# Projections, kv and num of a fused attention and feed-forward kernel in stationary tiles of 32 columns

## The chip, the cores and the metric

One core of a Trainium2 chip runs the whole program. The metric is the device time of one execution in microseconds. A second number of the same kind is the time of one execution that the hardware profiler recorded; the trace and all views of the profile come from that one execution.

## The reference

Linear attention with random features, followed by a gated feed-forward layer, all in float32. There are 8 batches with 8 heads, 576 positions a head, 64 numbers a head and 128 random features:

```python
def phi(x):                                   # x = q * scale or k * scale
    proj = np.einsum('bhsd,md->bhsm', x, omega)
    sq = np.sum(x * x, axis=-1, keepdims=True) / 2.0
    h = proj - sq
    h = h - np.max(h, axis=-1, keepdims=True)
    return np.exp(h) / np.sqrt(m)
q_p, k_p = phi(q_s), phi(k_s)
kv = np.einsum('bhsm,bhsd->bhmd', k_p, v)
z = np.sum(k_p, axis=2)
num = np.einsum('bhsm,bhmd->bhsd', q_p, kv)
den = np.einsum('bhsm,bhm->bhs', q_p, z)[..., None] + 1e-06
...
out = ((x @ w_a) * (x @ w_b)) @ w_out         # x = num / den, 4608 x 512, d_ff = 1536
```

## The kernel before, in words

**Two kinds of work on TensorE.** The feed-forward layer takes most of it. Its matmuls use the full array, 128 rows by 128 stationary columns, with each number split into a high and a low part; lines 1057, 1127, 1247 and 1340 in the profile are these. Between them stand short bursts of attention work in plain float32, for one pair of heads at a time (32 pairs in all, 4 per batch). The change touches these bursts.

**Projections.** The queries and keys of a pair lie with the 64 numbers of a head on the partitions: one head on partitions 0 to 63 and the other on 64 to 127, positions along the free dimension. A chunk is 128 positions. `four` (line 573) projects four chunks and `eight` (line 593) eight chunks. The stationary operand is a piece of the queries or keys, 64 rows by 64 positions; the moving operand is `om`, omega transposed, 64 rows by 128 features, once on each half of the partitions. For each chunk there are four matmuls: two halves of the positions (`t`), whose results go to two halves of the PSUM partitions, by two heads (`w`), whose rows are the two halves of the array and whose results go to two PSUM banks. So the four fill the four 64x64 quarters of the array. The results, `ppk` and `ppq`, are read by ScalarE and VectorE in `scores`, which takes the maximum, the bias and the exponential.

**kv.** `kv_burst` (`kvmm`, line 848) sums over five chunks of positions. The stationary operand is 128 positions by the 64 numbers of `v` of one head, the moving operand the features of the keys, 128 columns. The two heads (`j`) go to the two halves of the PSUM partitions of one tile `pkv`, so a matmul takes 128 rows by 64 columns of the array, two side by side.

**num.** `num` (`mms`, lines 916 and 918) multiplies the transposed features of the queries with kv of the head. The stationary operand is kv, 128 features by 64; the moving operand is 512 positions (`pm`, line 916) and the last 64 positions (line 918, into the columns of the next pair's `pkv` or, standing alone, into `pt`). Again two heads side by side in two halves of the array. In the pairs of the first batch, which go through `tok_tail` instead, kv and num are done in another way that the change does not touch.

**What sets the order.** The whole program is a graph of operations (`Graph`). A planner simulates the engines with a price for each operation and so writes out one order for every engine ahead of time; buffers come from rings, and a seeded search shifted due times. The price of these bursts on TensorE is `mm4(n, cols)`, for n chunks or sums of so many moving columns: `n * 2 * max(110, 0.825 * cols)` ns. `TURNS` adds a price for each change between the three modes of the array ("f" for the full array, "r" for the projections, "c" for kv and num). num's matmuls are attached to the next pair's `kv_burst` (`front["mm"]`), so that both stand in one burst; two nums stand alone (`alone`). All loads and stores of data are issued from SyncE's queue except a few.

Of the kernel before, what the change touches and what calls it, by code (L numbers as in the profile page):

```python
# [19 lines left out]
P = 128  # L20
B, H, S, D, M = 8, 8, 576, 64, 128
# [9 lines left out]
TL = S - SM  # L31
# [5 lines left out]
SQ = SQ2 ** 0.5  # L37
EPS = 1e-6 * M
KS = NHP

CFG = dict(PORT=0.5, EDF=("DVE", "ACT", "POOL"), STEP=15000, LOOK=60000, NOISE=(200, 600), CHOSEN=((858009,0,387055,152612,0,0,0,715321,0,0,680034,0,0,0,0,780129,689749,0,892332,0,0,84647,0,0,0,0,0,0,0,0,0,0,0,0,0,0,0,0,0,0,0,0,0,0,0,0,0,0,0,0,0,0,0,0,0,0,0,0,0,0,0,0,0,0,0,0,0,0,0,0),), ZS=800, ZB=(300, 1600, 3600), ZD=(300, 1600, 3100), HQ=(1100, 2600, 3600), BACK2=(300, 1100, 2600), TW=(), XL=["v0", "v1", "Xt0", "ht2", "hq0"], OWR=["raw0", "raw1"], ONE=((7, 1),), SAFE=500, OWN=16, OWNU=(), HOLD=1000, TG=1, G4=4, WAIT=150, RAW=600, FAST=(0, 1, 2, 3), JOIN0=False, WARM=8, HROOM=["w0", "u1", "w1", "u2", "w2", "u3"], H=3, TURN=(7,), BACK=1500, AT=2, GATES=(-4, -1, 2, 5), SQPE=4, MARGIN=1200, LOAD=1100, SUMS=1000, NATS=(1, 2, 3), CONV=(28000, 2600))

# [291 lines left out]
def mm4(n, cols):  # L334
    return n * 2 * max(110, 0.825 * cols)
# [6 lines left out]
def act(n):  # L342
    return 165 + 0.86 * n
# [11 lines left out]
def tile_attention_moe(ctx: ExitStack, tc: tile.TileContext, kqt, kqtt, kqn, kqnt, vx, omst, idn, wab, wout, out):  # L355
    nc = tc.nc
# [11 lines left out]
    for name, n in dict(X=2, Xw=0, nat=2, x2=0, v=2, hk=1, hq=2, qd=1, kvz=0, sm=3, sq=3, ht=3, Xt=1, xl=0, xts=2, rd=2, x=4, xa=2, xf=2, Sa=2, Sb=2, st=0,  # L368
                        w=NF, u=NF, t=0, tst=0, wo=3, raw=2, a=2, c=0, bq=0, ghl=2, osb=0, ot=0, owr=0, og=0, ogf=0, oc=0, zs=1, z2=1, zb=2, k2=2, kl=1, dn=1, tails=0, zq=2, zx=2,
# [14 lines left out]
    def fixed(shape, dtype, name):  # L384
        b = g.buf(None, shape, dtype, name)
        b.ap = const.tile(shape, dtype, name=name)
        return b
# [3 lines left out]
    def copier(o, i, scale=None):  # L391

        def go(e):
            if e == "ACT":
                nc.scalar.copy(o(), i())  # L395
            elif e == "DVE":
                nc.vector.tensor_copy(o(), i())
            else:
                nc.gpsimd.tensor_scalar(o(), i(), 1.0, 0.0, op0=ALU.mult, op1=ALU.add)
        return go  # L400
# [9 lines left out]
    om = fixed([P, M], F32, "om")  # L410
    ind = fixed([P, P], F32, "ind")
    for k in range(4):
        g.op({"POOL": 110}, lambda e, k=k: nc.gpsimd.memset(ind.ap[D * (k // 2):D * (k // 2) + D, D * (k % 2):D * (k % 2) + D], SQ2 * (k in (0, 3))),
             w=[(ind, k)], prio=-5000)
# [103 lines left out]
    def split(b, hp, src, sbuf, pri, al=(), gate=()):  # L518

        xt = xmain[b, hp]  # L520
        n = HM if xt.half else SM
        g.op({"ACT": act(n)}, copier(lambda: xt.at(0), lambda: src()[:, 0:n]), r=[sbuf], w=[xt.part(0)], alloc=list(al), prio=pri, deps=gate)
        if b >= B1:
            sums(b, hp, src, sbuf, pri, gate)
        g.op({"DVE": dve(n)}, subber(lambda: xt.at(1), lambda: src()[:, 0:n], lambda: xt.at(0)), r=[sbuf, xt.part(0)], w=[xt.part(1)], prio=pri)
# [38 lines left out]
    def four(nm, b, pri, x, xdep, dst, c0, sm, sq, al, deps, mg, more):  # L564

        pps = [g.buf("at", [P, 4 * M], F32, f"pp{'kq'[w]}{nm}{c0}", more) for w in range(2)]

        def go(e):
            for c in range(4):
                for t in range(2):  # L570
                    for w in range(2):
                        rows, half = slice(D * w, D * w + D), slice(D * t, D * t + D)
                        nc.tensor.matmul(pps[w].ap[half, c * M:c * M + M], x()[rows, c * P + D * t:c * P + D * t + D], om.ap[rows], start=True, stop=True)  # L573
        lead = g.op({"PE": mm4(4, M)}, go, r=[*xdep, (om, None)], w=[(pp, "p") for pp in pps], alloc=[*pps, *al], prio=pri, deps=deps, margin=mg, mode="r")
        flat = [lambda pp=pp: pp.ap for pp in pps]
        scores(nm, b, pri, x, xdep, dst, c0, sm, sq, flat, [[(pp, "p")] for pp in pps], more)
        return lead

    def eight(nm, b, pri, x, xdep, dst, sm, sq, al, deps, mg, room):

        pps = [g.buf("at", [P, 4 * M], F32, f"pp{'kq'[w]}{nm}") for w in range(2)]
        own = [] if room else [g.buf("ab", [P, 2, HM], F32, f"pp{'kq'[w]}b{nm}") for w in range(2)]
        room = room or own
        banks = [pps, room]
        flat = [[lambda t=t: t.ap for t in pps], [lambda t=t: t.ap.rearrange("p h n -> p (h n)") for t in banks[1]]]
        parts = [[[(t, "p")] for t in pps], [[(t, 0), (t, 1)] for t in banks[1]]]

        def go(e):
            for c in range(8):
                for t in range(2):  # L590
                    for w in range(2):
                        rows, half = slice(D * w, D * w + D), slice(D * t, D * t + D)
                        nc.tensor.matmul(flat[c // 4][w]()[half, c % 4 * M:c % 4 * M + M], x()[rows, c * P + D * t:c * P + D * t + D], om.ap[rows], start=True, stop=True)  # L593
        lead = g.op({"PE": mm4(8, M)}, go, r=[*xdep, (om, None)], w=[d for half in parts for p in half for d in p], alloc=[*pps, *own, *al],
                    prio=pri, deps=deps, land=mg, late=room, mode="r")
        for i in (1, 0):
            scores(nm, b, pri + 5 * (1 - i), x, xdep, dst, 4 * i, sm, sq, flat[i], parts[i], ())
        return lead
# [101 lines left out]
    def first_k(gate):  # L700

        u, mg = KS, CFG["MARGIN"]
        b, hp = divmod(u, NHP)
# [131 lines left out]
    def kv_burst(u, pri, hk, vb, mg):  # L835

        b, hp = divmod(u, NHP)
        nm, he = f"_{b}_{hp}", ends[b]
        heads = kv_chunks(hk, hp, he[0])
        front = pending.pop() if pending else None  # L840
        pkv = g.buf("at", [P, M + TL], F32, f"pkv{nm}")
        k2 = g.buf("k2", [P, M], F32, f"k2{nm}")

        def kvmm(e):
            for n in range(5):
                for j in range(2):
                    c, vc = heads[j][n]
                    nc.tensor.matmul(pkv.ap[D * j:D * j + D, 0:M], vb.ap[:, vc, 0:D], c(), start=(n == 0), stop=(n == 4))  # L848
            if front:
                front["mm"](pkv)  # L850
        g.op({"PE": mm4(5, M) + (front["cost"] if front else 0)}, kvmm, r=[(vb, None), (hk, None), (he[0], hp), *(front["r"] if front else ())],
             w=[(pkv, None), *(front["w"] if front else ())], alloc=[pkv, k2, *(front["alloc"] if front else ())], prio=pri, margin=mg, mode="c")
        if front:
            front["rest"](pkv)
        g.op({"ACT": act(M)}, copier(lambda: k2.ap[:], lambda: pkv.ap[:, 0:M]), r=[(pkv, None)], w=[(k2, None)], prio=pri)
        return k2
# [52 lines left out]
    def num(u, pr, hq, qT):  # L909
        b, hp = divmod(u, NHP)  # L910
        nm, pri = f"_{b}_{hp}", pr + 140
        pm = g.buf("at", [P, SM], F32, f"pm{nm}")

        def mms(pt):
            for j in range(2):
                nc.tensor.matmul(pm.ap[D * j:D * j + D], qT[0](j), qT[1](j), start=True, stop=True)  # L916
            for j in range(2):
                nc.tensor.matmul(pt.ap[D * j:D * j + D, M:M + TL], qT[0](j), qT[2](j), start=True, stop=True)

        def rest(pt):  # L920

            split(b, hp, lambda: pm.ap[:], (pm, None), pri)
            ends_out(b, hp, lambda: pt.ap[:, M:M + TL], pt, pri)
        pending.append(dict(mm=mms, rest=rest, cost=mm4(1, SM) + 120, r=qT[3], w=[(pm, None)], alloc=[pm, *xmain[b, hp].new], u=u, pri=pri))
# [9 lines left out]
    def kv_chunks(hk, hp, hke):  # L934

        main = [[(lambda c=4 * j + n: hk.ap[:, c], 6 * j + n) for n in range(4)] for j in range(2)]
        return [main[j] + [(lambda: hke.ap[:, hp], 4 + j)] for j in range(2)]
# [79 lines left out]
        ends_out(b, hp, lambda: pt.ap[:, 0:TL], pt, pr + 160)  # L1017


    steps = []  # L1020
    MOE = 10 ** 6
    spare = []
# [413 lines left out]
    def attention(u, room=None):  # L1436

        gate = steps[-1:] if u >= 2 * NHP else turned[CFG["G4"]:] if u == NHP else []
        if u == KS:
            first_k(gate)  # L1440
        if u < KS:
            pair(u, gate)
# [43 lines left out]
def lay(q, k, v, omega, w_a, w_b, w_out):  # L1486
# [25 lines left out]
    lay = main.copy()  # L1512
    lay[KS:NU - 1, :D] = main[KS + 1:, :D]
    for j in range(2):
        lay[NU - 1, D * j:D * j + D, :SM] = main[KS, :D, SM * j:SM * j + SM]
        lay[NU - 1, D * j:D * j + D, SM:] = main[NU - 1, D:, SM * j:SM * j + SM]
# [33 lines left out]
```

## Time and profile before

| what | value |
|---|---|
| median of 3 runs | 1043.05 us (1042.86 to 1043.57) |
| the profiled execution's own time | 1043.14 us |
| its span, from the first instruction to the last | 1041.3 us |
| mean granted clock of TensorE | 0.999 |
| TensorE busy | 1029.7 us, 8958 matmul records |
| VectorE busy | 887.5 us |
| ScalarE busy | 598.7 us |
| GpSimd busy | 114.3 us |
| moved by DMA | 314.31 MB, mean 302 GB/s |

In the profile PE is TensorE's matmul, PEld its weight load, DVE is VectorE, ACT ScalarE, POOL GpSimd and SP SyncE. A row of the groups gives line, engine, operation, tiles (written <- read), the part of the array (rows*columns), the operands' shape and the count, then the busy time in us and the mean time of one in ns, then idle time before them and who ended it. A row of the timeline gives the start in us from the span's start, the duration in us, and the same names. A duration of a matmul holds its way through the array, so that many overlap; what they cost in sequence is seen from start to start. PEclk is the granted clock in tenths, 9 being 90% or more.

### The profile page before, as it was taken

The numbers are of one execution on the slowest core, as the hardware profiler recorded it, in microseconds if no ns is written. First come the engines' busy times: TensorE is split into PE (matmuls) and PEld (weight loads), VectorE is DVE, ScalarE is ACT, GpSimd is POOL, SyncE is SP. The second block draws the span as 40 slices with busy tenths as digits, with TensorE's granted clock in tenths as the row PEclk, the third lists the DMA queues.
The fourth block names the chain that finished last, engine by engine and source line by source line (L and its number), as shares of the span: only waits on it lengthen the run. The fifth ranks groups of instructions, "written<-read, shape, count | busy, mean of one in ns | idle before, by whom it ended". The sixth has DMA issues, their size and how long they took to land.

```text
span 1041.3 us, 24378 instructions
## 1 busy us (share of the span) xinstructions
PE 1029.7 (99%) x8958; PEld 906.2 (87%) x8958; DVE 887.5 (85%) x2212; ACT 598.7 (57%) x1656; POOL 114.3 (11%) x181
## 2 busy tenths in 40 slices
PE   9999999999999999999999999999999999999998
PEld 8877777777788888988888888988899899999998
DVE  6999999899999788879887978888877579998766
ACT  7997798777675665566565656665554123332211
POOL 0032211121111111111101111111110000000000
PEclk9999999999999999999999999999999999999999
DMA  9787878999899998899989998988887888999981
GB/s 356 279 298 245 282 242 288 302 345 313 299 341 365 309 317 293 306 342 306 307 276 354 311 303 293 337 302 304 276 285 268 278 314 310 314 348 335 375 307 45
DMA packets 123656, 314.31 MB, mean 302 GB/s; under 512 B 17680, under 2 KB 40976, under 8 KB 123536
## 3 DMA queue, kind: packets, MB, share of 16 engines
q1 hardware_dynamic: 122656, 312.10, 86.5%
q8 instruction: 70, 1.15, 0.4%
q10 hardware_dynamic: 880, 0.66, 0.2%
q14 instruction: 50, 0.41, 0.1%
HBM read 255.52 MB, written 57.18 MB: 300 GB/s over the span
## 4 chain that ended last, share of the span: by engine, by line
PE 81%; DVE 6%; ACT 1%; DMA 1%; issue 0%; DVEq 0%; ACTq 0%
PE p L1340 38%; PE o L1057 20%; PE o_P L1127 4%; PE pa L1247 4%; PE pb L1247 4%; PE pkv L848 3%; PE pm L916 2%; PE ppk L593 1%; PE p L593 1%; DVE c L1350 1%; DVE sm L626 1%; PE ppk L573 1%; PE p L1127 1%; DMA t<-td 1%; PE ppke L573 1%
## 5 line engine op out<-in xcount | busy, mean ns | idle before, releaser
L1350 DVE TENSOR_TENSOR c<-p,c 128x512 f32<-128x512 f32 (+1 forms) x336 | 207.4, 617 | 68.2 <-PE p L1340 59.5
L1057 PE MATMUL o<-wo,ghl 128*128 128x512 f32 x1008 | 258.7, 397 | 0.4 <-DVE ghl L403 0.3
L1057 PEld LDWEIGHTS o<-wo,ghl 128*128 128x128 f32 x1008 | 181.0, 188 | 39.7 <-issue 4.6
L1340 PE MATMUL p<-Sa,t 128*128 128x256 f32 x1008 | 132.6, 281 | 0.0
L1340 PEld LDWEIGHTS p<-Sa,t 128*128 128x128 f32 x1008 | 124.6, 188 | 0.4 <-issue 0.2
L801 POOL TENSOR_TENSOR z<-hk 128x256 f32<-128x256 f32 x56 | 45.1, 806 | 606.0 <-ACT hk L639 429.6
L395 ACT CAST ghl<-c 128x512 fp32r<-128x512 f32 (+1 forms) x75 | 42.5, 579 | 100.5 <-DVE c L1400 79.8
L877 ACT ACTIVATE hq<-hq,dn 128x128 f32<-128x128 f32 x224 | 71.0, 391 | 28.5 <-DVE dn L873 28.2
L867 DVE CUSTOM_DVE_ANT_0 zero<-hq,zb 128x128 bf16<-128x128 f32 x224 | 80.3, 358 | 4.9
L1247 PE MATMUL pa<-x,wa 128*128 128x512 f32 x288 | 74.9, 401 | 2.2 <-ACT a L395 1.0
L1340 PE MATMUL p<-Sb,bq 128*128 128x256 f32 x504 | 74.1, 283 | 0.0
L1340 PE MATMUL p<-x,t 128*128 128x256 f32 x504 | 73.9, 282 | 0.0
L1340 PE MATMUL p<-Sb,t 128*128 128x256 f32 x504 | 73.5, 282 | 0.0
L395 ACT COPY c<-p 128x256 f32<-128x256 f32 x84 | 31.3, 372 | 73.2 <-PE p L1340 62.4
L1247 PE MATMUL pb<-x,wb 128*128 128x512 f32 x288 | 73.0, 397 | 0.3 <-DVE a L1255 0.3
L1340 PEld LDWEIGHTS p<-x,wa 128*128 128x128 f32 x504 | 64.8, 188 | 7.2 <-DVE c L1350 3.7
L1340 PE MATMUL p<-x,wa 128*128 128x256 f32 x504 | 68.2, 283 | 2.0 <-DVE c L1350 1.0
L639 ACT ACTIVATE hq<-hq,sm 128x128 f32<-128x128 f32 x192 | 65.3, 392 | 7.4 <-DVE sm L634 6.1
L1247 PEld LDWEIGHTS pa<-x,wa 128*128 128x128 f32 x288 | 52.8, 188 | 17.6 <-ACT a L395 1.9
L1340 PEld LDWEIGHTS p<-x,wb 128*128 128x128 f32 x504 | 64.6, 188 | 3.8 <-DVE c L1350 0.6
L1340 PE MATMUL p<-x,wb 128*128 128x256 f32 x504 | 67.8, 282 | 0.1
L1340 PEld LDWEIGHTS p<-x,t 128*128 128x128 f32 x504 | 65.7, 189 | 1.5 <-DVE c L1350 0.4
(209 smaller groups left out, 2028.8 us busy)
## 6 DMA issues: line engine op xcount, KB each, us to landing
t<-td SPq DMA_DIRECT2D x168, 512.0 KB
wo<-wod SPq DMA_DIRECT2D x96, 512.0 KB
bq<-bd SPq DMA_DIRECT2D x84, 256.0 KB
qdr<-qd SPq DMA_DIRECT2D x112, 160.0 KB
hq<-qdr SPq DMA_DIRECT2D x28, 640.0 KB
X<-in_kqt_dram SPq DMA_DIRECT2D x30, 512.0 KB
raw<-in_wab_dram SPq DMA_DIRECT2D x24, 512.0 KB
td<-ts SPq DMA_DIRECT2D x24, 512.0 KB
```

Source lines behind the costliest of these rows:

```text
L395: nc.scalar.copy(o(), i())
L573: nc.tensor.matmul(pps[w].ap[half, c * M:c * M + M], x()[rows, c * P + D * t:c * P + D * t + D], om.ap[rows], start=True, stop=True)
L639: g.op({"ACT": 392}, lambda e, c=c, w=w, to=to, at=at: nc.scalar.activation(to.ap[:, at + c], src[w](c), AF.Exp, scale=SC, bias=sm.ap[:, 2 ...
L801: g.op({"POOL": pool2(n)}, lambda e: nc.gpsimd.tensor_tensor(o(), a(), c(), op=ALU.add), r=r, w=w, alloc=list(al), prio=pri, deps=zload[-1 ...
L848: nc.tensor.matmul(pkv.ap[D * j:D * j + D, 0:M], vb.ap[:, vc, 0:D], c(), start=(n == 0), stop=(n == 4))
L867: g.op({"DVE": 413}, lambda e, c=c, j=j, rr=rr, qc=qc: nc.vector.tensor_tensor_reduce(out=junk.ap[rr], in0=qc(), in1=zb.ap[rr, j], scale=1 ...
L877: g.op({"ACT": 392}, lambda e, c=c, src=src: nc.scalar.activation(hq.ap[:, c], src(), AF.Copy, scale=dn.ap[:, c:c + 1]), r=[sd, (dn, None) ...
L1057: nc.tensor.matmul(po.ap[:], ghl.ap[:, gi, t * P:(t + 1) * P], wo.ap[:, wi], start=(n == 0 and i == 0), stop=(n == NF - 1 and i == 2))
L1127: nc.tensor.matmul(pb.ap[:, t], A[0](ai)[:, t * P:(t + 1) * P], W[0](wi), start=begin and t == j == 0, stop=stop and t == 1 and j == 2)
L1247: nc.tensor.matmul(pb.ap[:], wt.ap[:, wi, c], xs[c].at(xi), start=(c == 0 and i == 0), stop=(c == NC4 - 1 and i == 2))
L1340: nc.tensor.matmul(pb.ap[:, half], wcol(wi, c), xc(xi, c), start=n == 0, stop=n == 5)
L1350: g.op({"DVE": dve(n)}, lambda e: nc.vector.tensor_tensor(c4.ap[:, o], pb.ap[:, half], y(), op=ALU.add), r=[*((pb, k) for k in range(half. ...
```

## The change

The stationary operand of these matmuls is cut into pieces of 32 columns (`Q = 32`) instead of 64. In `four` and `eight`, `t` steps over four quarters of the 128 positions instead of two halves, so a chunk takes eight matmuls of 64 rows by 32 columns. In kv and num a list `parts` holds the two heads by two halves of the 64 numbers, so that each step takes four matmuls of 128 rows by 32 columns. The moving operands, the results and their places in PSUM are the same. The prices of the planner are left as they were.

```diff
+Q = 32
...
         def go(e):
             for c in range(4):
-                for t in range(2):
+                for t in range(0, P, Q):
                     for w in range(2):
-                        rows, half = slice(D * w, D * w + D), slice(D * t, D * t + D)
-                        nc.tensor.matmul(pps[w].ap[half, c * M:c * M + M], x()[rows, c * P + D * t:c * P + D * t + D], om.ap[rows], start=True, stop=True)
+                        rows = slice(D * w, D * w + D)
+                        nc.tensor.matmul(pps[w].ap[t:t + Q, c * M:c * M + M], x()[rows, c * P + t:c * P + t + Q], om.ap[rows], start=True, stop=True)
...
             for c in range(8):
-                for t in range(2):
+                for t in range(0, P, Q):
                     for w in range(2):
-                        rows, half = slice(D * w, D * w + D), slice(D * t, D * t + D)
-                        nc.tensor.matmul(flat[c // 4][w]()[half, c % 4 * M:c % 4 * M + M], x()[rows, c * P + D * t:c * P + D * t + D], om.ap[rows], start=True, stop=True)
+                        rows = slice(D * w, D * w + D)
+                        nc.tensor.matmul(flat[c // 4][w]()[t:t + Q, c % 4 * M:c % 4 * M + M], x()[rows, c * P + t:c * P + t + Q], om.ap[rows], start=True, stop=True)
...
         def kvmm(e):
             for n in range(5):
-                for j in range(2):
+                for j, d in parts:
                     c, vc = heads[j][n]
-                    nc.tensor.matmul(pkv.ap[D * j:D * j + D, 0:M], vb.ap[:, vc, 0:D], c(), start=(n == 0), stop=(n == 4))
+                    nc.tensor.matmul(pkv.ap[D * j + d:D * j + d + Q, 0:M], vb.ap[:, vc, d:d + Q], c(), start=(n == 0), stop=(n == 4))
...
         def mms(pt):
-            for j in range(2):
-                nc.tensor.matmul(pm.ap[D * j:D * j + D], qT[0](j), qT[1](j), start=True, stop=True)
-            for j in range(2):
-                nc.tensor.matmul(pt.ap[D * j:D * j + D, M:M + TL], qT[0](j), qT[2](j), start=True, stop=True)
+            for j, d in parts:
+                nc.tensor.matmul(pm.ap[D * j + d:D * j + d + Q], qT[0](j)[:, d:d + Q], qT[1](j), start=True, stop=True)
+            for j, d in parts:
+                nc.tensor.matmul(pt.ap[D * j + d:D * j + d + Q, M:M + TL], qT[0](j)[:, d:d + Q], qT[2](j), start=True, stop=True)
...
+    parts = [(j, d) for j in range(2) for d in range(0, D, Q)]
```

## The prediction

> **What bounds the kernel now.** I read the page first, then the groups of instructions by line, the rows of the changed lines alone, and at last single instructions in the timeline. The page says who sets the end:
>
> ```profile
> span 1041.3 us, 24378 instructions
> PE 1029.7 (99%) x8958; PEld 906.2 (87%) x8958; DVE 887.5 (85%) x2212; ACT 598.7 (57%) x1656; POOL 114.3 (11%) x181
> ...
> PEclk9999999999999999999999999999999999999999
> ...
> PE 81%; DVE 6%; ACT 1%; DMA 1%; issue 0%; DVEq 0%; ACTq 0%
> ```
>
> TensorE is busy 99% of the span, holds 81% of the chain that ended last, and its granted clock is full in every slice. So a nanosecond more or less of TensorE's time is about a nanosecond of the span, wherever it falls. The question is how long the changed matmuls keep TensorE, so I look at one burst of them. These are the matmuls of one call of `four` (line 573) with their neighbours; columns are start in us, duration, engine, line, operation, tiles, shape of the array's tile, operand shape:
>
> ```profile
> 228.74 0.40 PE L1247 MATMUL pa<-x,wa 128*128 128x512 f32 x1
> 229.06 0.32 PE L573 MATMUL ppke<-om,Xe 64*64 64x128 f32 x1
> 229.07 0.32 PE L573 MATMUL ppqe<-om,Xe 64*64 64x128 f32 x1
> 229.08 0.32 PE L573 MATMUL ppke<-om,Xe 64*64 64x128 f32 x1
> 229.08 0.32 PE L573 MATMUL ppqe<-om,Xe 64*64 64x128 f32 x1
> 229.22 0.27 PE L573 MATMUL ppke<-om,Xe 64*64 64x128 f32 x1
> 229.23 0.27 PE L573 MATMUL ppqe<-om,Xe 64*64 64x128 f32 x1
> 229.24 0.27 PE L573 MATMUL ppke<-om,Xe 64*64 64x128 f32 x1
> 229.24 0.27 PE L573 MATMUL ppqe<-om,Xe 64*64 64x128 f32 x1
> 229.33 0.27 PE L573 MATMUL ppke<-om,Xe 64*64 64x128 f32 x1
> ...
> 229.77 0.27 PE L573 MATMUL ppke<-om,Xe 64*64 64x128 f32 x1
> ...
> 229.88 0.27 PE L573 MATMUL ppke<-om,Xe 64*64 64x128 f32 x1
> ...
> 229.90 0.27 PE L573 MATMUL ppqe<-om,Xe 64*64 64x128 f32 x1
> 230.10 0.50 PE L1247 MATMUL pa<-x,wa 128*128 128x512 f32 x1
> ```
>
> They go in sets of four, one for each 64x64 quarter of the array, and the sets follow every 0.11 us (229.22, 229.33, ... 229.77, 229.88: 0.66 us for six steps). The burst has 16 matmuls in the program and 32 rows here, so each matmul is two passes, eight sets in all. The four quarters are all at work: there is no empty corner of the array that narrower tiles could fill. Before the change 64 rows x 64 columns x 4, after it 64 x 32 x 8: the same area. The useful work per set is equal, and this is the first and strongest reason to expect little.
>
> **Part 1, the steady sets.** How much time do the changed lines take? The rows of each line alone over the whole span, in the order 573 (`four`), 593 (`eight`), 848 (kv), 916 and 918 (num and its tail); only the counts in brackets matter:
>
> ```profile
> 0.00:1042.00 1042.00, 36.12 (x1024) 28.89 (x1024) 1.00 0.87 302
> 0.00:1042.00 1042.00, 40.42 (x1280) 35.32 (x1280) 1.00 0.87 302
> 0.00:1042.00 1042.00, 36.76 (x560) 30.00 (x560) 1.00 0.87 302
> 0.00:1042.00 1042.00, 28.89 (x112) 6.97 (x112) 1.00 0.87 302
> 0.00:1042.00 1042.00, 7.96 (x112) 8.04 (x112) 1.00 0.87 302
> ```
>
> The projections have 1024 + 1280 = 2304 passes, 576 sets of four: 576 x 0.11 = 63.4 us. In bursts: 1024/32 = 32 calls of `four` and 1280/64 = 20 of `eight`. kv has 560 passes in sets of two (128x64 halves), 28 bursts of ten sets; one of them, with the matmul behind it:
>
> ```profile
> 61.15 1.09 PE L848 MATMUL pkv<-hk,v 128*64 128x128 f32 x16
> 62.07 0.39 PE L848 MATMUL pkv<-htk,v 128*64 128x128 f32 x4
> 62.39 0.96 PE L1057 MATMUL o<-wo,ghl 128*128 128x512 f32 x3
> ```
>
> From 61.15 to 62.39 is 1.24 us: 0.16 for a first set as above, 0.20 behind the last, and eight steps of 0.11 between. So kv is 280 x 0.11 = 30.8 us. num's streams are longer:
>
> ```profile
> 107.68 0.39 PE L848 MATMUL pkv<-htk,v 128*64 128x128 f32 x4
> ...
> 107.90 1.03 PE L916 MATMUL pm<-hq,kl 128*64 128x512 f32 x4
> ...
> 108.76 0.28 PE L918 MATMUL pkv<-hq,kl 128*64 128x64 f32 x4
> ...
> 108.97 0.50 PE L1247 MATMUL pb<-x,wb 128*128 128x512 f32 x1
> ```
>
> From 107.90 to 108.76 is 0.86 us for two sets, 28 times: 24 us; the tail 0.21 us to 108.97, 28 times: 6 us. Some 124 us of TensorE's time are touched. After the change every set has twice as many passes over the same moving columns, each on its own strip. If all strips stream at once, a set lasts 0.11 us as now and the term is 0. That each pass still takes its 0.11 us I take from the moving operand, which is not changed (128 columns, 512 for num).
>
> The condition is that TensorE can start the eight passes within one set. In the rows above, four pairs of weight load and pass start from 229.22 to 229.24: three steps in 0.02 us, 6.7 ns each. Eight need 7 x 6.7 = 47 ns, under half of 110. That is the price I take, because it is measured on the same kind of pass, on different tiles. The bound on the other side is the fastest pace that the trace shows kept up: four in 110 ns, 27.5 ns each; at that pace a set of eight would take 220 ns, and the projections would cost 63.4 us more. kv and num have four passes a set after the change, as the projections have now, so by either price they fit.
>
> The Trainium skill ("TensorE: Matmul & The Clock Gate", Part 1) speaks against this change: it states that matmuls never start closer than about 25 ns to one another, however short. An estimate from that page's figure: 576 sets x (8 x 25 - 110) ns = 52 us more, 1095 us. The 6.7 ns steps above disagree with it for passes on different tiles, but the kept-up 27.5 ns does not, so the trace of before does not settle it.
>
> **Part 2, head and tail of a burst.** At the head the first set has to wait for its weights: 229.06 to 229.22 is 0.16, against 0.11 for a hidden load. That is 50 ns, which fits the widths, line 593's loads of 64 columns against line 1340's of 128:
>
> ```profile
> L1340 PEld LDWEIGHTS p<-Sa,t 128*128 128x128 f32 x1008 | 124.6, 188 | 0.4 <-issue 0.2
> L593 PEld LDWEIGHTS p<-om,X 64*64 64x64 f32 x544 | 15.9, 133 | 0.0
> ```
>
> 188 - 133 = 55 ns for 64 columns; so 32 columns fewer load 27 ns sooner. All four first passes have 0.32 us instead of 0.27, so their loads ran side by side and I let eight do so too. Gain: 27 ns at each burst. At the tail the last set starts its last pass 7 steps after the first instead of 3: 4 x 6.7 = 27 ns later, and the next line's matmul waits for the end of that (229.90 to 230.10). For the 52 projection bursts head and tail cancel. kv, num and its tail run as one burst (107.68 to 108.97 shows no switch of tile shape), with only 2 more steps at its end: -27 + 13 = -14 ns, 30 times at most (28 kv bursts and two nums alone, 112/4 = 28 nums): -0.4 us. Inside bursts the loads are hidden now (rows of the second set) and are shorter after. The bounds of this part: heads alone, (52 + 30) x 27 = -2.2 us; tails alone, 52 x 27 + 30 x 13 = +1.8 us.
>
> **Part 3, what I cost at nothing.** The order: the planner's price of each operation (`mm4`) is not changed, so the planned order, the buffers and the DMAs stay. No wait is added; the readers of a bank wait for its last pass, which comes at the same time within the 27 ns above. Accumulation in kv keeps its ten sets, on narrower strips. The program grows by 3088 passes and 3088 loads (1024 + 1280 + 560 + 112 + 112), which have to be fetched:
>
> ```profile
> q8 instruction: 70, 1.15, 0.4%
> q14 instruction: 50, 0.41, 0.1%
> ```
>
> q8's 1.15 MB over TensorE's 2 x 8958 instructions is 64 bytes each, and a packet (1.15 MB / 70 = 16.4 KB) holds 256 of them: one call of `eight` after the change. 6176 more are 24 packets. What hides them is that a packet now lasts 15 us on average and `eight` takes 1.8; if that cover failed, a packet's own time (0.4% x 16 x 1041 / 70 = 0.95 us, engines' time each) would be bared at up to 20 bursts, 19 us. The chain shows no share for TensorE's sequencer now, though bursts eat half a packet in 1.8 us, so I take 0.
>
> **Sum.** 0 + 0 - 0.4 us. Against the profiled execution's own 1043.14 us (span 1041.3, so 1.8 us lie outside it): 1042.7 us. The median of the three runs, 1043.05, is 0.1 lower, which I neglect. A measurement of this kernel can tell about 0.2%, 2.1 us, from no change; this is well within.
>
> **Rivals.**
>
> *A, slower: TensorE cannot start eight passes in a set.* The limit is its issue of instructions, which must bring 16 in 110 ns where it brings 8 now, or how far it looks past a pass that waits for its own tile. It costs from the point at which a step takes more than 110/8 = 13.8 ns. In part (16 ns a step): 576 x (128 - 110) = 10.4 us, 1053. In full (27.5): 63.4 us, 1106. For it: no stretch of the trace keeps up more than four in 110 ns, since nothing asked for it. Against it: the 6.7 ns steps, and that one pass's load already starts beside others. Chance 0.22, of which 0.13 up to 1065 and 0.09 above. The page's rule of part 1 is this case nearly in full (by its figure 1095), and has no chance beyond that 0.09.
>
> *B, slower: the moving operand cannot be read by four column strips at once.* Today two strips of the array read the same partitions; after it four. If two is the most, projections, kv and num all double: 63.4 + 30.8 + 24 + 6 = 124 us, 1167; a loss of a tenth would be 12 us, 1055. For it: nothing here uses four strips. Against: a set lasts 0.11 us in kv, with 128 rows in two strips, as in the projections, with two halves of 64 rows in two strips each, so no shared limit shows yet. Chance 0.09, half of it below 1065.
>
> *C, faster: the switch of tile shape gets shorter as well.* A burst begins 0.32 us after the last matmul of 512 columns (228.74 to 229.06) and the next matmul begins 0.20 us after its last pass, 0.09 beyond the 0.11 of its stream. If a narrower tile drains or loads in half of this 0.09 too, and tails do not grow: 82 x (27 + 45) ns = 5.9 us, 1037.2. For it: 82 such switches, all bare. Against: the rows after the burst belong to 128-column tiles, which don't change. Chance 0.10.
>
> **How the numbers follow.** Forecast (eight at once, within 0.2%, 1041.0 to 1045.1): 0.58. A 0.22, B 0.09, C 0.10, and 0.01 for a bared fetch of instructions. So faster 0.10, same 0.58, slower 0.32. The forecast's own range is 1040.9 to 1044.9, from the bounds of part 2. To leave out no more than 2 in 10, the range goes down to 1039.0 (most of C) and up to 1065.0 (the partial forms of A and B): 0.58 + 0.13 + 0.05 + 0.06 = 0.82.
>
> **What would show it.** Right: lines 573 and 593 with 4608 passes of 64*32, starting in eights every 0.11 us; their loads near 106 ns; the first set of a burst 0.13 us long instead of 0.16; kv in fours every 0.11 us; the chain's shares as now. Wrong by A: sets of eight spread over 0.13 to 0.22 us while kv keeps 0.11. Wrong by B: kv's and num's sets longer too (107.90 to 108.76 above 0.86 us). Wrong by C: 230.10 closer than 0.20 us to the last pass.

## The result, and the profile after

The changed kernel takes 1055.76 us (median of 6 runs, 1053.18 to 1058.9) against 1043.15 us before (6 runs, 1042.86 to 1043.57): a ratio of 1.0123, 95% interval 1.0106 to 1.0141. It is slower by 12.6 us. The forecast was 1042.7 us, no change; the result lies in the range for the partial forms of rivals A and B, but neither of them is the cause. A first sign of something else is the spread: 5.7 us from run to run after, 0.7 us before. The profiled execution is the slowest of the six, 1058.9 us with a span of 1057.1, so in the trace 15.8 us are to be found.

The page after, the rows that answer to those of before:

```profile
span 1057.1 us, 30554 instructions
PE 1036.0 (98%) x12046; PEld 908.2 (86%) x12046; DVE 887.6 (84%) x2212; ACT 599.3 (57%) x1656; POOL 114.8 (11%) x181
...
q8 instruction: 94, 1.54, 0.6%
...
PE 82%; DVE 11%; issue 2%; ACT 2%; DMA 2%; DVEq 0%; ACTq 0%; SPq 0%
```

"issue", time in which an engine waited for nothing that the profile shows, was 0% of the chain and is 2% now. TensorE fetches 94 packets of instructions instead of 70. VectorE's share of the chain rose from 6 to 11% though its busy time is the same (887.5 and 887.6 us), so the shares alone do not tell the cause.

**The bursts themselves** did nearly what was forecast. Here is a call of `four` in the timeline, start and duration in us, the first set of eight and parts of the later ones:

```profile
62.84 0.29 PE L574 MATMUL ppke<-om,Xe 64*32 64x128 f32 x1
...
62.89 0.29 PE L574 MATMUL ppqe<-om,Xe 64*32 64x128 f32 x1
62.97 0.27 PE L574 MATMUL ppke<-om,Xe 64*32 64x128 f32 x1
...
63.08 0.27 PE L574 MATMUL ppke<-om,Xe 64*32 64x128 f32 x1
...
63.41 0.27 PE L574 MATMUL ppke<-om,Xe 64*32 64x128 f32 x1
63.42 0.27 PE L574 MATMUL ppqe<-om,Xe 64*32 64x128 f32 x1
63.43 0.27 PE L574 MATMUL ppke<-om,Xe 64*32 64x128 f32 x1
63.44 0.27 PE L574 MATMUL ppqe<-om,Xe 64*32 64x128 f32 x1
63.46 0.27 PE L574 MATMUL ppke<-om,Xe 64*32 64x128 f32 x1
63.48 0.27 PE L574 MATMUL ppqe<-om,Xe 64*32 64x128 f32 x1
63.49 0.27 PE L574 MATMUL ppke<-om,Xe 64*32 64x128 f32 x1
63.51 0.27 PE L574 MATMUL ppqe<-om,Xe 64*32 64x128 f32 x1
```

Eight start in 0.05 us, the first set lasts 0.13 us, the next sets 0.11 (62.97, 63.08). From the sixth set on the eight are spread over 0.10 us of the set (63.41 to 63.51), with some 17 ns between most of them, while the first of each set still comes every 0.11. The end of the burst:

```profile
63.73 0.27 PE L574 MATMUL ppqe<-om,Xe 64*32 64x128 f32 x1
63.93 0.50 PE L1249 MATMUL pb<-x,wb 128*128 128x512 f32 x1
```

So from 62.84 to 63.93 the burst takes 1.09 us, where it took 1.04 (229.06 to 230.10 before). By the same reading `eight` is 0.08 us longer. kv takes 1.23 us instead of 1.24, and num's two sets 0.85 instead of 0.86:

```profile
68.95 1.08 PE L849 MATMUL pkv<-hk,v 128*32 128x128 f32 x32
69.84 0.40 PE L849 MATMUL pkv<-htk,v 128*32 128x128 f32 x8
70.18 0.50 PE L1059 MATMUL o<-wo,ghl 128*128 128x512 f32 x1
```

```profile
115.66 1.04 PE L917 MATMUL pm<-hq,kl 128*32 128x512 f32 x8
116.51 0.29 PE L919 MATMUL pkv<-hq,kl 128*32 128x64 f32 x8
```

Sum: 32 x 53 + 20 x 79 - 30 x 13 ns = 2.9 us (differences of single starts and ends, finer than the rows print). That leaves some 12.9 of the 15.8 us.

**The rest stands in the waits.** Who ended TensorE's idle times, total us, times, longest; the first six rows after (before, "issue" had none):

```profile
PE ppk L574 <- issue: 3.2, 1, 3.2
PE o L1059 <- issue: 2.4, 1, 2.4
PE ppke L574 <- issue: 1.7, 1, 1.7
PE pa L1249 <- ACT a L396: 1.0, 2, 0.7
PE ps L616 <- issue: 1.0, 1, 1.0
PE pkv L979 <- issue: 1.0, 1, 1.0
```

Five times TensorE stands still for over a microsecond without a semaphore to blame, in the middle of an operation as well as between two. The longest:

```profile
14.90 0.27 PE L574 MATMUL ppq<-om,X 64*32 64x128 f32 x1
18.41 0.27 PE L574 MATMUL ppk<-om,X 64*32 64x128 f32 x1 [3.24 <-issue]
```

From start to start the five are 1.3, 3.5, 1.2, 2.8 and 1.9 us (from 10.8, 14.9, 37.8, 464.3 and 694.7 us): 10.8 us. Counting TensorE's recorded instructions from the first, weight loads, matmuls and semaphore instructions alike, 449, 705, 1473, 11713 and 17601 are done when it stops: each is 193 more than a multiple of 256, the size of a packet. The DMA view shows the packet that is waited for. In the first 1.1 us of the long stall no packet of q8 moves; in the next 1.1 us one does:

```profile
q1 hardware_dynamic: 218, 0.42, 99.2%
q8 instruction: 1, 0.02, 5.4%
```

By the record of that packet it begins at 16.09 and takes 0.96 us, and TensorE goes on 1.4 us after its end. At all five stops it goes on 1.2 to 1.5 us after the end of a packet.

The rest is the clock. The stretches of the two longest stalls and behind them; the column ahead of the last two is the granted clock:

```profile
14.90:18.40 3.50, 0.27 (x16) 0.00 (x0) 0.33 (x1) 1.90 (x8) 0.00 (x0) 1.00 1.05 408
18.40:21.00 2.60, 2.59 (x23) 2.39 (x22) 2.06 (x5) 0.34 (x2) 0.00 (x0) 0.76 1.03 419
21.00:23.20 2.20, 2.20 (x12) 2.20 (x12) 0.49 (x3) 0.60 (x4) 0.00 (x0) 0.51 1.03 412
464.30:467.10 2.80, 0.42 (x3) 0.02 (x1) 1.79 (x5) 0.52 (x2) 0.00 (x0) 0.96 0.88 259
467.10:472.00 4.90, 4.90 (x81) 3.87 (x82) 1.03 (x4) 1.72 (x6) 0.00 (x0) 0.67 0.48 150
```

After the longest stall the clock was 0.76 over 2.6 us and 0.51 over the next 2.2, after the second longest 0.67 over 4.9 us, with TensorE busy: 0.6 + 1.1 + 1.6 = 3.3 us at most. Compared one by one with themselves before, the matmuls that the change leaves alone fall 1.5 us further behind from 18.8 to 22.9 us and 1.4 us from 467.1 to 470.1: 2.9 us lost. The three terms, 2.9 + 10.8 + 2.9 = 16.6 us, are 0.8 more than the 15.8: the 10.8 still holds the ordinary step at each stop, and some of the delay is made up where TensorE waited before (0.2 us at 105.5 us, for instance).

### The profile page after: what moved, and what is told of

Its sections match the earlier page's. It is cut to its first block, busy times and chain, and to the rows that moved or that the text cites. A ratio compares the mean times of both kernels' runs of the same rounds, so it can differ in the third digit from the quotient of the medians.

```text
span 1057.1 us, 30554 instructions
## 1 busy us (share of the span) xinstructions
PE 1036.0 (98%) x12046; PEld 908.2 (86%) x12046; DVE 887.6 (84%) x2212; ACT 599.3 (57%) x1656; POOL 114.8 (11%) x181
## 4 chain that ended last, share of the span: by engine, by line
PE 82%; DVE 11%; issue 2%; ACT 2%; DMA 2%; DVEq 0%; ACTq 0%; SPq 0%
PE p L1342 38%; PE o L1059 19%; PE o_P L1129 4%; PE pa L1249 3%; PE pb L1249 3%; PE pkv L849 3%; PE pm L917 2%; DVE zero L868 1%; PE p L594 1%; PE ppk L594 1%; PE ppk L574 1%; DVE sm L627 1%; DVE c L1352 1%; DVE raw L450 1%; PE pkv L979 1%
```

## The experiments

**Theory F (fetch).** TensorE's instructions come in packets of 256. In the changed kernel a call of `four` uses up half a packet (128) in 0.9 us and a call of `eight` a whole one in 1.8 us, where a packet of the kernel before lasted 15 us on average. Where bursts lie close together, a packet is used up before the next has come. **Theory S (strips).** The eight narrow strips are slow themselves, and the stops are waits between engines that follow from it.

**The parts alone.** Four kernels, each with the change at some places:

- e1: `four` and `eight` as changed; `kvmm` and `mms` as before
- e2: `kvmm` and `mms` as changed; `four` and `eight` as before
- e3: `four` as changed; the rest as before
- e4: `eight` as changed; the rest as before

> Tiles of 32 columns in the projections alone (four and eight); kv and num as before. Theory F (fetch: TensorE's instructions come in packets of 256, and a packet that is used up in under about 4 us is gone before the next has come): most of the loss stays, 1050 to 1057 us, with idle times of 1 to 4 us ahead of TensorE instructions whose place in the program is the same modulo 256 in each case. Theory S (the eight column strips themselves run slower): 1046 us, from bursts that are 53 ns (four) and 79 ns (eight) longer, 32 x 53 + 20 x 79 = 3.3 us, and no long idle times.

Measured: 1060.61 us, ratio 1.017 (1.0156 to 1.0184). Slower than the whole change and 3.6 us above what theory F gave, though it has fewer instructions. Counted as above, eight stops of 0.7 to 3.5 us, 13.4 us, all with 193 over a multiple of 256. Without kv's and num's extra instructions the packets are cut at other places, and more of them fall on bursts. Theory S as the whole cause (1046) falls.

> Tiles of 32 columns in kv and num alone; the projections as before. Both theories: the bursts get 13 ns shorter, 30 x 13 = 0.4 us, so 1042.7 us. Theory F adds nothing much, since these bursts bring only 672 more passes and as many loads, 5 packets, and none of them uses a packet up in under 4 us: no idle time over 1 us that the kernel before has not. Were the four column strips slow, kv and num would show it here: 1045 us or more.

Measured: 1042.72 us, ratio 0.9998 (0.9989 to 1.0007), no such stop; its shortest packet lasts 6.3 us. The gain of 0.4 us that was forecast is too small to be told from nothing; four strips cost nothing that can be measured.

> Tiles of 32 columns in four alone. Theory F: the start holds most calls of four close together, so the stalls of the first 50 us stay, if not at the same places since the packets are cut elsewhere later on: 1047 to 1054 us. Theory S: 32 x 53 ns = 1.7 us, 1044.8 us.

Measured: 1055.18 us, ratio 1.0122 (1.0106 to 1.0137): just above theory F's range. `four` alone costs as much as the whole change. Four stops, 7.6 us, at 11.1, 15.0, 37.9 and 215.0 us. After the second and the fourth (3.8 and 2.3 us) the clock was again at one half, and the unchanged matmuls lost some 3 us there, a cost that theory F does not name.

> Tiles of 32 columns in eight alone. Theory F: nothing before 220 us, then a stall of 1 to 3 us wherever two bursts fall into one packet: 1045 to 1052 us, the first 200 us as in the kernel before. Theory S: 20 x 79 ns = 1.6 us, 1044.7 us.

Measured: 1046.71 us, ratio 1.0036 (1.0025 to 1.0048). One long stop, inside a call of `eight`:

```profile
680.04 0.72 PE L594 MATMUL p<-om,X 64*32 64x128 f32 x33
682.62 0.38 PE L594 MATMUL p<-om,X 64*32 64x128 f32 x2 [1.86 <-issue]
682.93 0.51 PE L1058 MATMUL o<-wo,ghl 128*128 128x512 f32 x1
```

A short one of 0.4 us comes at 624.1 us, also in a call of `eight`; both are 193 over a multiple of 256. The stops (2.1 and 0.4 us) and 20 x 79 ns are 4.1 us of the 4.2 by which its span is longer (1045.5 against 1041.3). The parts don't add up to the whole (e3 and e4 together would be 16 us), since each edit moves every later cut.

**The same number of instructions without narrow strips.** Tiles of 64 columns, and the moving operand in two halves:

```diff
                 for t in range(2):
-                    for w in range(2):
+                    for n in range(0, M, D):
+                        for w in range(2):
...
-                        nc.tensor.matmul(... [half, c * M:c * M + M], ..., om.ap[rows], ...)
+                            nc.tensor.matmul(... [half, c * M + n:c * M + n + D], ..., om.ap[rows, n:n + D], ...)
```

> The projections keep stationary tiles of 64 columns, and the moving operand is cut into two halves of 64 columns instead: as many passes and instructions as with tiles of 32 columns, in the four quarters of the array as before. kv and num as before. Theory F and the count of instructions: bursts as short of instructions as in the first experiment, so idle times of 1 to 4 us at packet ends again and 1050 to 1062 us; the order and the places in the program are those of the first experiment. Theory S (the narrow strips): no strips, so 1043 us, or with weight loads that are not hidden 1045 us, and no idle times over 1 us that the kernel before has not.

Measured: 1064.05 us, ratio 1.0204 (1.0182 to 1.0226). Its waits, the first rows:

```profile
PE ppk L574 <- issue: 5.8, 2, 3.5
PE ppqe L574 <- issue: 1.3, 1, 1.3
PE p L595 <- issue: 1.2, 2, 1.0
PE ppke L574 <- issue: 1.2, 2, 0.6
```

Eight stops, 12.1 us, among them those at 11.2, 15.4, 216, 471, 526 and 700 us, where the first experiment has its own. So it is the count of instructions, not the shape of the tile. The bursts are longer here, too (`four` by 105 ns, `eight` by 165: 6.7 us), with sets of four passes every 58 ns, which is more than the 2 us by which it lies above the range.

**The cuts moved, and nothing else.** Tiny matmuls ahead of the first burst, behind line 425 of the changed kernel, 18 or 32 of them (in e9 18, in the kernel before):

```diff
+        for _ in range(18):
+            nc.tensor.matmul(none.ap[0:2, 0:2], zero.ap[:, 0:2], zero.ap[:, 0:2], start=True, stop=True)
```

> The kernel before with the same 18 tiny matmuls. Both theories: within 0.2% of the kernel before, so that the tiny matmuls themselves are shown to cost nothing; by theory F because no packet of it is used up in under 4 us wherever it is cut.

Measured: 1043.46 us, ratio 1.0003 (0.9993 to 1.0012), no stop; its shortest packet lasts 6.4 us. The tiny matmuls cost nothing that can be measured.

> The changed kernel with 18 tiny matmuls (2 by 2 columns) ahead of the first burst, while TensorE waits for omega: 36 instructions, which move every later instruction by 36 places against the packets of 256. Theory F: by the changed kernel's own trace without its stalls, nine packets would be used up in under 3.8 us instead of four, and the sum by which packets stay under 4.5 us grows from 6.8 to 14.4 us: 1060 to 1070 us, with the idle times at other places in time but at the same place modulo 256. Theory S and every theory of waits between engines: 1056 us, idle times at 10.8, 14.9, 37.8, 464 and 695 us as before.

Measured: 1062.2 us, ratio 1.0175 (1.016 to 1.019): in theory F's range, 6.4 us above the changed kernel. Its waits:

```profile
PE p L596 <- issue: 4.7, 3, 2.4
PE ppk L576 <- issue: 2.8, 1, 2.8
PE ppq L576 <- issue: 2.5, 1, 2.5
PE pn L994 <- issue: 1.9, 1, 1.9
```

Seven stops, 14.1 us, at 9.3, 18.5, 38.9, 326.6, 467.8, 526.4 and 700.2 us: other instructions than before, and again 193 over a multiple of 256 although 36 more stand ahead. A wait between engines would have stayed with its instruction.

> As the kernel with 18 tiny matmuls, but 32: 64 places. Theory F: six packets under 3.8 us, the sum under 4.5 us 8.8 us: 1056 to 1062 us, idle times near 6 to 9, 27, 345, 369, 511, 682 and 709 us instead of the old places. Theory S: 1056 us and the old places.

Measured: 1062.53 us, ratio 1.0181 (1.0166 to 1.0196): 0.5 us above the range. Ten stops, 14.7 us. The forecast places had been counted without stalls, so most come later. Of the seven, five came, by their packets at 9, 35.5, 359, 385 and 699 us; those forecast for 511 and 709 us did not. Five came unforecast, at 18, 24, 327, 469 and 617 us. There the packets used up before the stops had lasted up to 6.3 us, and in e6 one of 6.1 us stopped, while one of 2.3 us in e6 (726 us) did not. So there is no sharp limit at 4 us: how short a packet is tells that it is in danger, and whether it stops depends on when the next one's transfer begins as well.

Theory F so has the cause and the kind of place right, but not the size: four of its eight forecasts were too low (e1, e3, e5 and e8).

## Why the prediction was wrong, point by point

- **What bounds the kernel** was right: TensorE is 82% of the chain, and each stop of it is a stop of the whole.
- **Part 1, steady sets: right.** Eight passes start in each 0.11 us, in kv and num four; term 0. Rival A's longer sets (128 or 220 ns) did not come, and rival B is refuted altogether (1.23 us for kv, 0.85 for num). That 1055.8 us lies where their partial forms would have put it is chance. The rule of the Trainium skill that spoke against the change ("TensorE: Matmul & The Clock Gate", Part 1, starts not under about 25 ns) does not hold for passes on different tiles: eight in 109 ns, 13.6 ns each, were kept up over whole calls of `eight`.
- **Part 2, head and tail: the head right, the tail mis-sized.** Loads take 105 ns for 133, the first set 0.13 us, as forecast. The tail was taken from the 6.7 ns between starts at the head of a burst and came out as 47 ns; from the sixth set on the eight are spread over some 100 ns. For kv and num the forecast of -14 ns a burst held (16 ns shorter in the trace). 53 and 79 ns a burst instead of 0: +2.9 us in place of -0.4, outside the bounds that part 2 gave (+1.8). The row used as price showed a pace that was not kept up. What sets the wider spacing no run took apart.
- **Part 3, "so I take 0" for the fetch of instructions: this step failed.** The count was right to the packet (24 more). The cover was not: "a packet now lasts 15 us on average" is a mean over stages. In the first 50 us of the kernel before 588 matmuls and 588 loads are 4.6 packets, 11 us each, and inside that stage calls of `four` follow each other directly. The shortest packet before, counted along its trace, lasts 7.8 us; in the changed kernel the one used up before the stop at 14.9 us lasts 2.8. The part had the mechanism and its price (19 us at worst, at 0.95 us a stop; measured are 1.2 to 3.5 us a stop, and the half clock behind the two longest) and gave it a chance of 0.01. The sign that it looked for, a share of TensorE's sequencer in the chain, is not there after the change either: the waiting shows as "issue". The reason against it, that bursts already ate half a packet in 1.8 us without harm, says nothing of a whole one. The Trainium skill ("Runtime: NRT & Kernel Launch", Instruction fetch mechanics) states that instructions come in blocks of 256, the next fetched while the current one runs, and that crossing costs little since an engine issues more slowly than the fetch fills. The block size agrees with the runs; that the crossing costs little does not, at five crossings of the changed kernel (10.8 us).
- **Rival C** did not come: the next matmul still starts 0.20 us behind the last pass.

Shown are the cause of the stops (count and cut of the instructions) and the length of the bursts. Open is why a packet's transfer begins up to 4.3 us (in e6 6.6 us) after the one before it has begun to be used. In the long stall all 16 DMA engines were full (103.7% as the view gives it, for q1 over 14.5 to 18.5 us), which fits waiting behind data, but no run with less traffic was tried.

## What to carry to other kernels

Doubling the instructions of work that already filled the array gained nothing here (e2) and cost up to 21 us (e5): work out how long a packet of 256 instructions lasts in the densest stage, not on average, and compare it with the time in which one was seen to come (here a transfer of about 1 us, 1.2 to 1.6 us until the engine goes on, and up to 4.3 us, once 6.6, before it begins). Idle times with "issue" and no releaser, at the same place modulo 256, are the sign. A spread from run to run is a weak one: the kernel before spread over 3.0 us in 17 runs, and e1, with eight stops, over 1.7 in four. A change of a few instructions anywhere ahead then moves the time by several us, so small edits to such a kernel are compared with the cuts in mind.

## What was not expected of the hardware

- After the stops at 14.9 and 464 us (3.5 and 2.8 us) the granted clock was one half for 3.4 us by the clock's own record, which cost 1.4 to 1.5 us more than the stop itself. The same followed ten stops of 2.3 to 3.8 us in the other runs, but not two of 2.3 and 2.6 us in e6 (467.8 and 526.4 us). In all traces the clock's record changes only at whole steps of 3.41 us from its first entry (steps 4, 5, 135 and 136 in the changed kernel). With the traces cut at these steps, TensorE stood idle for at least 1.8 us of the step ahead of every half clock; after a step with 1.7 us or less none followed, nor after one with 1.9 in e6. The stop of 2.6 us in e6 lies across two steps (1.4 and 1.0 us idle). So where a stop falls decides as well as how long it is.
- The first eight passes of a burst start within 0.05 us, and the next eight follow 0.13 us behind the first, which suggests that a matmul's second pass does not hold up the matmuls on other tiles. In which order the passes stand in the program no view shows.
- Passes that start 6.6 ns apart at the head of a burst are mostly some 17 ns apart from the sixth set on, though the sets keep their 0.11 us.
